# Routed attention and an MLP mixer on one core: attention in units of four heads by half the queries

## The chip, the cores and the metric

The kernel runs on one core of a Trainium2 chip. A core has a matrix engine (TensorE, PE in the profile), a vector engine (VectorE, DVE), a scalar engine (ScalarE, ACT), GpSimd (POOL), and SyncE (SP), which issues most transfers here. Operands lie in an on-chip memory of 128 partitions. Matmuls write to eight banks of a second memory (`ps` in the code), from which DVE and ACT read. The metric is the device time of one execution in microseconds (us). The kernel before takes 802.99 us, the median of three runs from 802.93 to 803.22.

## The reference

There are two blocks, one behind the other. The first is attention with routing: B = 4 batches, H = 8 heads, S = 768 positions, head dimension 64, 16 centroids for each head. Each query and key is assigned to its best centroid, and a query sees only the keys of its own cluster:

```python
q_assign = np.argmax(np.einsum('bhsd,hcd->bhsc', q_n, c_n), axis=-1)
k_assign = np.argmax(np.einsum('bhsd,hcd->bhsc', k_n, c_n), axis=-1)
mask = q_assign[:, :, :, None] == k_assign[:, :, None, :]
scores = scale * np.matmul(q, k.transpose(0, 1, 3, 2))
scores = np.where(mask, scores, -1000000000.0)
scores = scores - np.max(scores, axis=-1, keepdims=True)
attn = np.exp(scores)
attn = attn / (np.sum(attn, axis=-1, keepdims=True) + 1e-09)
return np.matmul(attn, v).astype(np.float32)
```

The heads are put side by side to x, 768 positions by 512 channels for each batch. The second block is an MLP mixer: `h = relu(x^T w_tok1) w_tok2` over positions, `u = x + h^T`, then `u + relu(u w_ch1) w_ch2` over channels. The weights come in 64-bit floats; the kernel gets them as pairs of 32-bit words and rounds them itself.

## The kernel before, in words

**Work and its order.** Everything is one straight program, and all tiles are stretches of one large buffer, `arena`. The program is first recorded as operations (class `Program`, lines 72 to 226), each with its cost, with what it reads and writes, and with the engines that may do it. Then `plan` lays out an order for every engine: PE keeps the order in which its operations were recorded; every other engine takes the operation that is ready and has the earliest due time, by the costs in the code. SP's transfers are ordered in the same way. On the chip each engine then goes through its own list strictly in order, and waits for semaphores where an operation needs another engine's result. So a planner's cost that differs from the chip's time changes no order, only who waits.

**Attention** goes in 16 units (`pair(m)`, line 1282), one for two heads. Both heads of a pair lie beside each other: 64 partitions each.

- *Load.* `load_qkr` fetches queries and keys, `part_qk` (ACT, line 870 through `halves`) splits them into high and low halfwords, SP transposes these by DMA (line 905), and `join_qk` (ACT) puts them together into `Ts`: head dimension on partitions. The first three pairs are transposed on PE instead (`turn_qk`).
- *Route* (line 1068): PE multiplies by the centroids (four column groups of 32), DVE takes the largest of each 16 (lines 1085 to 1090), ACT makes of it rows of 0 and 1 and rows of 0 and minus a large number, and counts hits (line 1094). Through a small DRAM tile these rows become the mask operands `Ms`, so that one bf16 matmul adds a large negative number to each score outside the cluster.
- *Scores* (line 1147): 12 chunks, each one key tile of 128 keys by half the queries (384), for both heads. For each head there is one f32 matmul (64 rows by 128 columns of the array, the two heads in two row groups) and one bf16 matmul with the mask; they leave the result in two banks. ACT takes the exponential of both heads at once (line 1190, 768 numbers in each partition) into `exs`. Three pairs of banks take turns. DVE adds the six key tiles up in two sums (`tt`, line 880, 1536 numbers).
- *Values* (line 1218): for each of six key tiles 16 f32 matmuls: two heads, two halves of the head dimension, and four groups of 32 queries, each group in a column group of its own (line 1207). The sums of the exponentials come in the same way (`sums`).
- *Finish* (line 1246): DVE turns sums and values back (lines 1249 and 1263), takes the reciprocal and multiplies.

The operations of PE in a pair follow each other as scores, four key tiles of values, the route of the pair after the next, two more key tiles with the sums.

**The mixer** follows: token products by a Strassen-like scheme (seven products in place of eight), then channel products by two levels of it. Their weights are rounded in 31 pieces (`weight_round`, line 1306: DVE lines 1326 to 1336, and `tt`), which may begin at START + STEP x n us, lie beside the attention, and go to DRAM. A check of ranges at the end reads the weights once more (`weights_in_range`, ACT line 1863) and counts (`check`). A second, general path is taken only if the check fails.

The code as it stands, with its line numbers:

Of the kernel before, what the change touches and what calls it, by code (L numbers as in the profile page):

```python
# [9 lines left out]
F32 = mybir.dt.float32  # L10
# [9 lines left out]
C = 16  # L20
# [40 lines left out]
HOLD = {"DVE": 0.15}  # L61
# [5 lines left out]
START, STEP = 14, 13  # L67


class Op:  # L70
    __slots__ = ("opts", "fn", "preds", "succs", "left", "ready", "end", "due", "seq", "eng", "lat", "bytes", "after", "port", "first_lat", "mode")


class Program:
# [10 lines left out]
    def add(self, opts, fn, rd=(), wr=(), size=None, after=0.0, mode=None):  # L85
# [3 lines left out]
        o.lat, o.mode = 0.0, mode  # L89
# [27 lines left out]
    def run(self):  # L117
# [602 lines left out]
def kernel(  # L720
# [38 lines left out]
    wdm = [dram.tile([P, HS], BF16, name=f"wdm{i}") for i in range(2)]  # L759
# [19 lines left out]
    araw = buf(75, [768, 2], U32)  # L779
# [4 lines left out]
    vs = [buf(15 + 3 * i, [2, NJ, D]) for i in range(3)]  # L784
    Ts = [buf(24 + 6 * i, [NQK, P]) for i in range(3)]
    Ms = [buf(42 + 3 * i, [2, S], BF16) for i in range(2)]
    M0 = buf(102, [2, S], BF16)
    heads = Buf(arena, 330, [2])
    msc0 = Buf(arena, 332, [2, 2])
    exs = [buf(48 + 6 * i, [2, S]) for i in range(6)] + [buf(96, [2, S])]  # L790
    es = [buf(84 + 6 * i, [2, S]) for i in range(2)]
    denT = buf(105, [HS])
    rt = [buf(106.5 + 1.5 * i, [HS]) for i in range(3)]

    qkr = buf(9, [2, 2, NJ, D])
    qka = [buf(3 + 3 * i, [2, NJ, 2, D], U16) for i in range(2)]
    qkt = [buf(111 + 3 * i, [NQK, P], U16) for i in range(2)]
    rb = buf(117, [HS], BF16)
    nsq = buf(118, [P])
    mxs = buf(118.5, [32])  # L800
    hits = Buf(arena, 672, [32])

    O = buf(119, [8, 2, 2, W])
    Os = buf(127, [4, 7, W])
    raws = [buf(134 + 4 * i, [WMAX, 2], U32) for i in range(3)]
    tmps = [[buf(146 + 6 * i + 2 * n, [WMAX], U32) for n in range(3)] for i in range(2)]
# [86 lines left out]
    def vec(fn, c, rd, wr):  # L893
        return g.add({"DVE": c - 0.08}, lambda e: fn(), rd, wr)
# [8 lines left out]
    def transpose(dst, src, rd, wr, kb):  # L903
        return g.add(
            {"SP": ISSUE}, lambda e: nc.sync.dma_start(dst, src, transpose=True), rd, wr,
            (1.3 * kb * 1024, 512),
        )


# [12 lines left out]
    def load_qkr(m, after=0.0):  # L922
# [1082 lines left out]
```

## Time and profile before

| | |
|---|---|
| median of three runs | 802.99 us |
| the profiled execution | 803.35 us |
| its span | 801.3 us |
| granted clock of PE, mean | 0.998 |
| PE busy | 785.5 us, 98% |
| DVE busy | 663.9 us, 83% |
| ACT busy | 468.0 us, 58% |
| POOL busy | 189.6 us, 24% |
| transfers | 143.70 MB, 70.0% of 16 DMA engines on the main queue |

A line of groups reads: code line, engine, operation, what is written and read, partitions by numbers of the form, count; then busy time and the mean of one in nanoseconds, then idle time before it with what ended it. PE's matmuls overlap, so the mean of one is longer than its share of the time. An f32 matmul of the code leaves two records (two passes), each with a weight load (PEld), a bf16 matmul one. The chain that ended last is given as start, length, and what was done.

### The profile page before, as it was taken

The page shows a single profiled execution, that of the slowest core. Times are in us where ns is not written, and L with a number is a line of the kernel's source. Part 1 is how long each engine was busy: PE and PEld are TensorE (multiplying, and loading weights), DVE is VectorE, ACT ScalarE, POOL GpSimd, SP SyncE. Part 2 cuts the span into 40 slices and gives each one's busy share as a digit, 9 for nine tenths or more (in the row PEclk, how much of TensorE's full clock was granted, in tenths as well). Part 3 has the DMA queues.
Part 4 walks back from the last instruction along what each step waited for, and adds up shares of the span by engine and source line. Part 5 has one row for each costly group of instructions (what it writes and reads, how often), then busy time and mean ns, then how long its engine had stood idle before and what let it go on. Part 6 is the DMA issues. An engine that isn't in the chain of part 4 may idle for free.

```text
span 801.3 us, 15484 instructions
## 1 busy us (share of the span) xinstructions
PE 785.5 (98%) x6063; PEld 467.3 (58%) x6063; DVE 663.9 (83%) x863; ACT 468.0 (58%) x615; POOL 189.6 (24%) x185
## 2 busy tenths in 40 slices
PE   8999999999999999999999999999999999999995
PEld 5566666666666666544555555555555555555553
DVE  6888788999999999999998767899852677799962
ACT  5588888888888875699623235434537605401332
POOL 0000000000000000001255599700285289810000
PEclk9999999999999999999999999999999999999999
DMA  8466666998999875689967855557987943333765
GB/s 186 159 170 152 146 159 170 219 211 186 227 234 202 188 217 129 146 159 203 196 182 209 246 182 177 185 179 199 253 246 199 262 120 101 103 103 98 178 155 136
DMA packets 264883, 143.70 MB, mean 179 GB/s; under 512 B 184160, under 2 KB 260704, under 8 KB 264800
## 3 DMA queue, kind: packets, MB, share of 16 engines
q1 hardware_dynamic: 262432, 141.83, 70.0%
q8 instruction: 50, 0.82, 0.4%
q10 hardware_dynamic: 2368, 0.79, 0.4%
q14 instruction: 33, 0.27, 0.1%
HBM read 91.95 MB, written 28.61 MB: 150 GB/s over the span
## 4 chain that ended last, share of the span: by engine, by line
PE 83%; DVE 10%; ACT 4%; issue 2%; POOL 0%; DVEq 0%; POOLq 0%; ACTq 0%
PE ps L841 68%; PE ps L1207 15%; DVE arena L880 7%; ACT arena L870 2%; ACT arena L1190 1%; DVE arena L1330 1%; DVE arena L1333 0%; DVE arena L1263 0%; DVE arena L1336 0%; ACT arena L860 0%; ACT arena L887 0%; DVE arena L1326 0%; DVE arena L1249 0%; DVE arena L862 0%; DVE arena L1085 0%
## 5 line engine op out<-in xcount | busy, mean ns | idle before, releaser
L841 PE MATMUL ps<-arena 128*128 128x384 f32 (+5 forms) x2735 | 641.3, 462 | 7.9 <-DVE arena L862 2.1
L841 PEld LDWEIGHTS ps<-arena 128*128 128x128 f32 (+1 forms) x2351 | 341.5, 185 | 252.8 <-issue 58.6
L880 DVE TENSOR_TENSOR arena<-arena 128x256 f32<-128x256 f32 (+6 forms) x340 | 354.1, 1062 | 22.9 <-ACT arena L1190 14.2
L880 POOL TENSOR_TENSOR arena<-arena 128x384 f32<-128x384 f32 x179 | 188.9, 1085 | 514.8 <-DVE arena L880 390.9
L880 DVE TENSOR_TENSOR arena<-ps,arena 128x384 f32<-128x384 f32 (+3 forms) x227 | 189.1, 843 | 88.7 <-PE ps L841 85.2
L870 ACT COPY arena<-arena 128x768 uint16<-128x768 uint16 x223 | 191.4, 948 | 47.9 <-DMA arena<-arena 22.3
L1190 ACT ACTIVATE arena<-ps 128x768 f32<-128x768 f32 x192 | 153.0, 810 | 32.4 <-PE ps L841 30.7
L1207 PE MATMUL ps<-arena 128*32 128x192 f32 (+1 forms) x3328 | 151.1, 339 | 0.0
L1207 PEld LDWEIGHTS ps<-arena 128*32 128x32 f32 x3328 | 106.5, 110 | 48.0 <-issue 20.3
L860 ACT COPY arena<-ps 128x1152 f32<-128x1152 f32 (+2 forms) x42 | 30.8, 738 | 105.4 <-PE ps L841 105.4
L887 ACT ACTIVATE arena<-arena 128x1152 f32<-128x1152 f32 (+1 forms) x38 | 40.2, 1076 | 55.5 <-DVE arena L880 54.1
L1863 ACT ACTIVATE arena<-arena 128x768 f32<-128x768 f32 x40 | 38.8, 969 | 56.4 <-DMA arena<-in_moe_w_tok_dram 30.7
L841 PEld LDWEIGHTS <-arena 64*128 64x128 bf16 x384 | 19.2, 94 | 25.0 <-DVE arena L1117 0.6
L1094 ACT ACTIVATE arena<-arena 128x384 bf16<-128x384 f32 x16 | 11.3, 708 | 19.7 <-ACT arena L870 9.5
L1336 DVE SCALAR_TENSOR_TENSOR arena<-arena 128x512 f32<-128x512 uint32 (+1 forms) x31 | 21.2, 684 | 0.7
L1330 DVE SCALAR_TENSOR_TENSOR arena<-arena 128x512 uint32<-128x512 uint32 (+1 forms) x31 | 20.7, 669 | 0.8
L1263 DVE STREAM_TRANSPOSE arena<-ps 128x768 f32<-128x768 f32 x16 | 15.6, 975 | 1.1 <-PE ps L1207 1.0
L1333 DVE TENSOR_SCALAR arena<-arena 128x512 uint32<-128x512 uint32 (+1 forms) x31 | 14.2, 457 | 0.5
L1085 DVE STREAM_TRANSPOSE arena<-ps 128x384 f32<-128x384 f32 x16 | 9.3, 580 | 4.7 <-PE ps L841 4.6
L1326 DVE TENSOR_SCALAR arena<-arena 128x512 uint32<-128x512 uint32 (+1 forms) x31 | 12.5, 403 | 0.0
L1249 DVE STREAM_TRANSPOSE arena<-ps 128x384 f32<-128x384 f32 x16 | 9.2, 577 | 3.0 <-PE ps L1207 2.9
L1090 DVE STREAM_TRANSPOSE arena<-arena 128x384 f32<-128x384 f32 x16 | 9.3, 578 | 0.6
(58 smaller groups left out, 49.6 us busy)
## 6 DMA issues: line engine op xcount, KB each, us to landing
arena<-wd SPq DMA_DIRECT2D x196, 192.0 KB, 2.5
wd<-arena SPq DMA_DIRECT2D x84, 224.0 KB, 3.7
arena<-in_moe_w_ch_dram SPq DMA_DIRECT2D x48, 256.0 KB, 4.8
arena<-in_moe_w_ch_dram SPq DMA_DIRECT2D x16, 768.0 KB, 4.4
arena<-in_v_dram SPq DMA_DIRECT2D x16, 384.0 KB, 5.1
out_dram<-arena SPq DMA_DIRECT2D x14, 384.0 KB, 3.8
arena<-in_k_dram SPq DMA_DIRECT2D x13, 384.0 KB, 3.9
arena<-in_q_dram SPq DMA_DIRECT2D x13, 384.0 KB, 4.3
```

The lines of the kernel that those rows point to most:

```text
L841: nc.tensor.matmul(dst, lhsT=lhsT, rhs=rhs, start=start, stop=stop, tile_position=pos, is_transpose=tr, skip_group_check=True,)
L860: nc.scalar.copy(out=dst, in_=src)
L870: nc.scalar.copy(out=dst, in_=src)
L880: (nc.vector if e == "DVE" else nc.gpsimd).tensor_tensor(out=dst, in0=a, in1=b, op=op)
L887: nc.scalar.activation(out=dst, in_=src, func=ACT.Relu)
L1190: lambda e, ex=ex, s=s, u=u: nc.scalar.activation(out=ex.ap[:, :, u * HS : (u + 1) * HS], in_=ps[:, 2 * s : 2 * s + 2, 0:HS], func=ACT.Exp ...
L1207: nc.tensor.matmul(dst, lhsT=lhsT, rhs=rhs, start=start, stop=stop, tile_position=pos, skip_group_check=True,)
L1263: lambda: nc.vector.transpose(out=x.ap[:, :, cols].rearrange("p j (c d) -> p c j d", d=32), in_=ps[:, 6:8, 0:HS],),
L1330: vec(lambda: nc.vector.scalar_tensor_tensor(out=TT, in0=hi, scalar=0xC0000000, in1=hh, op0=ALU.bitwise_and, op1=ALU.bitwise_or), 0.14 + 0 ...
L1333: vec(lambda: nc.vector.tensor_scalar(out=hh, in0=TT, scalar1=0xFF800000, scalar2=None, op0=ALU.bitwise_and), f, T.k(), h.k())
L1336: vec(lambda: nc.vector.scalar_tensor_tensor(out=ll, in0=lo, scalar=float(2.0**-52), in1=hh.bitcast(F32), op0=ALU.mult, op1=ALU.mult,), 0. ...
L1863: lambda e, i=i, func=func, bias=bias, n=n, hi=hi: nc.scalar.activation(out=hi, in_=hi, func=func, bias=bias, accum_out=wsum.ap[:, i, n : ...
```

## The change

It changes the units of attention from the third on. Pairs 0 and 1 stay as they are. Units 2 to 15 (`quad(t)`) each hold four heads of a batch and half of the queries; two units (w = 0 and 1) share the four heads n = t // 2.

- Queries and keys come as pieces (`load_piece`): half the positions of four heads, in rows of 768 bytes in place of 1536. `part_piece` also sorts them into blocks: 32 partitions for each head, the two halves of the head dimension (z) behind each other. Pieces 2 and 3 are sorted by copies and turned on PE (`turn_piece`, 12 transposes each), where before pair 2 alone was. Four tiles `Ts` in place of three.
- Scores (`scores_quad`): for a key tile, four row groups of 32, one head in each: two f32 matmuls (z = 0 and 1) and one bf16 mask matmul for each head, 384 queries, in four banks. Two exponentials follow, for two heads each, of the same size as before. Two sets of four banks take turns.
- Route (`route_quad`): once for four heads and all positions, in tiles of 64 rows by 32 columns, 16 matmuls, at the fifth key tile of even units. DVE's steps are done once on 768 numbers in place of twice on 384; the rows of the mask are now made by DVE, and ACT only counts. One transfer out and four in make a mask for four heads.
- Values (`values_quad`): for a key tile 32 matmuls of 96 columns in place of 16 of 192; they fill two banks of the half that the unit does not use for its last scores; sums go to a third bank there. `finish_quad` turns these out in two transposes.
- The planner's model: transfers cost by their packets, ACT may hold back 0.2 us for a more urgent operation, an operation can be given an earlier due time. Weight pieces may start every 9 us in place of 13; from the nineteenth piece on two load buffers in place of three, and one set of temporaries.
- The last range check has two load buffers in place of one, and `check` stands before the second group's first channel product.

```diff
-HOLD = {"DVE": 0.15}
+HOLD = {"DVE": 0.15, "ACT": 0.2}
...
-START, STEP = 14, 13
+START, STEP = 14, 9
...
-            o.bytes = size[0] * (1.2 if size[1] < 512 else 1.0)
+            o.bytes = BUS * size[0] / size[1] * (11 + 0.037 * size[1]) / 16e3
...
-                    o.due = min([s.due - 0.15 - lat for s in o.succs], default=total) - c
+                    o.due = min([s.due - 0.15 - lat for s in o.succs], default=total) - c - o.early
...
+    vq = [buf(15 + 6 * i, [4, NJ, D]) for i in range(2)]
+    Ts = [buf(at, [NQK, P]) for at in (39, 45, 27, 33)]
+    Ms = [buf(51 + 3 * i, [2, S], BF16) for i in range(2)]
+    exs = [buf(at, [2, S]) for at in (81, 87, 69, 75, 93, 57, 63)]
+    es = [buf(99 + 6 * i, [2, S]) for i in range(2)]
+    rt = [buf(112.5 + 3 * i, [2, HS]) for i in range(2)]
...
+    def load_piece(e, t, after=0.0):
+        n, w = divmod(e, 2)
+        b, hq = divmod(n, 2)
         for i, a in ((0, k), (1, q)):
             dma(
+                t.ap[:, 4 * i : 4 * i + 4].rearrange("p h j d -> p h (j d)"),
+                a[b, 4 * hq : 4 * hq + 4].rearrange("h (p j) d -> p h (j d)", p=P)[
+                    :, :, HJ * D * w : HJ * D * (w + 1)
+                ],
...
+    def turn_piece(e, banks):
+        t, R, T = rawq[e % 2], blk, Ts[e % 4]
+        src = t.ap.rearrange("p a j (z d) -> p z j a d", z=2)
+        for z in range(2):
...
+                    h.ap[:, z], src[:, z, n], S, qkr.k() + [("exps", e - 4)], h.rows(z, z + 1),
...
+    def join_piece(e):
...
+                    qkt[n].k() + [("exps", e - 3)], T.rows(r, r + NJ),
...
+    def assign(m, banks):
+        n = len(banks)
+        a, o, r = (Buf(arena, z.off, [n * HS], d) for z, d in zip((*rt, rb), (F32, F32, BF16)))
+        ak = a.k() + mxs.k()
+        src = ps[:, banks[0] : banks[-1] + 1 : max(1, banks[-1] - banks[0]), 0:HS]
...
+    def route_quad(n, banks):
+        hq = n % 2
+        parts = []
+        for z in range(2):
+            for p2 in range(2):
+                rows = slice(64 * p2, 64 * p2 + 64)
+                for gr in range(4):
+                    T = Ts[(2 * n + gr % 2) % 4]
+                    parts.append((
+                        ps[32 * gr : 32 * gr + 32, banks[p2], 0:HS], cbq.ap[rows, z, hq],
+                        blocks_of(T)[rows, z, :, 1 - gr // 2], z == 0, z == 1, (64 * p2, 32 * gr),
+                    ))
+        Tk = Ts[2 * n % 4].k() + Ts[(2 * n + 1) % 4].k()
+        mms(parts, 1.29, Tk + cbq.k(), bank(*banks), (64, 32))
+        assign(n + 1, banks)
+        dma(wdm, rb.ap, rb.k(), [("wdm",)], 192, 1536)
+        M = Ms[n % 2]
+        for h in range(4):
+            dma(
+                M.ap[32 * h : 32 * h + C].rearrange("c i (u n) -> c (i u) n", u=2),
+                wdm.rearrange("(g r) a n -> r g a n", g=4)[
+                    C * (h % 2) : C * (h % 2) + C, :, h // 2
+                ],
+                [("wdm",)] + M.k(), [("mq", n % 2, h // 2, h % 2)], 48, 768,
+            )
...
+    def scores_quad(t):
+        nonlocal nex
+        n, w = divmod(t, 2)
+        M, Tq = Ms[n % 2], Ts[t % 4]
+        st = unit[t] = [Buf(arena, exs[(nex + i) % len(exs)].off, [4, HS]) for i in range(NJ)]
+        nex += NJ
+        for i in range(NJ):
+            kw, kj = divmod(i, HJ)
+            Tk = Ts[(2 * n + kw) % 4]
+            s0 = 4 * ((i + t) % 2)
+            def rows(h):
+                return slice(32 * h, 32 * h + 32)
+            for z in range(2):
+                for p2 in range(2):
+                    mms(
+                        [
+                            (
+                                ps[:, s0 + h, 0:HS], blocks_of(Tk)[rows(h), z, kj, 0],
+                                blocks_of(Tq)[rows(h), z, :, 1], z == 0, False, (32 * h, 0),
+                            )
+                            for h in (2 * p2, 2 * p2 + 1)
+                        ],
+                        0.3225, Tk.k() + Tq.k(), bank(s0 + 2 * p2, s0 + 2 * p2 + 1), (32, P),
+                    )
+            for p2 in range(2):
+                mms(
+                    [
+                        (
+                            ps[:, s0 + h, 0:HS], M.ap[rows(h), 1, i * P : (i + 1) * P],
+                            M.ap[rows(h), 0, w * HS : (w + 1) * HS], False, True, (32 * h, 0),
+                        )
+                        for h in (2 * p2, 2 * p2 + 1)
+                    ],
+                    0.081, [("mq", n % 2, p2, h) for h in range(2)] + M.k(),
+                    bank(s0 + 2 * p2, s0 + 2 * p2 + 1), (32, P),
                 )
+            ex = st[i]
+            for p2 in range(2):
+                b0 = s0 + 2 * p2
+                g.add(
+                    {"ACT": 0.70},
+                    lambda e, ex=ex, b0=b0, p2=p2: nc.scalar.activation(
+                        out=ex.ap[:, 2 * p2 : 2 * p2 + 2], in_=ps[:, b0 : b0 + 2, 0:HS],
+                        func=ACT.Exp, scale=SM_SCALE,
+                    ),
+                    bank(b0, b0 + 1),
+                    ex.rows(2 * p2, 2 * p2 + 2)
+                    + ([("exps", t)] if i == NJ - 1 and p2 else []),
+                )
+        add_up(st)
...
+    def values_quad(t, i):
+        V, ex = vq[t // 2 % 2], unit[t][i]
+        b0 = 4 * (t % 2)
+        for p2 in range(2):
+            mms(
+                [
+                    (
+                        ps[32 * gr : 32 * gr + 32, b0 + p2, (2 * h + c) * 96 : (2 * h + c + 1) * 96],
+                        V.ap[:, 2 * p2 + h, i, 32 * c : 32 * c + 32],
+                        tokens(ex.ap[:, 2 * p2 + h], gr),
+                        i == 0 and h == 0 and c == 0, i == NJ - 1, (0, 32 * gr),
+                    )
+                    for h in range(2) for c in range(2) for gr in range(4)
+                ],
+                0.645, V.rows(2 * p2, 2 * p2 + 2) + ex.rows(2 * p2, 2 * p2 + 2), bank(b0 + p2),
+                (P, 32),
+            )
...
+    def finish_quad(t, bk):
+        n, w = divmod(t, 2)
+        b, hq = divmod(n, 2)
+        x, rcp = xs[b], rcps[t % 2]
+        vec(lambda: nc.vector.transpose(out=denT.ap, in_=ps[:, bk, 0:HS]), 0.57, bank(bk), denT.k())
...
+        js = slice(HJ * w, HJ * w + HJ)
+        b0 = 4 * w
+        for p2 in range(2):
+            cols = slice((2 * hq + p2) * P, (2 * hq + p2 + 1) * P)
+            vec(
+                lambda p2=p2, cols=cols: nc.vector.transpose(
+                    out=x.ap[:, js, cols].rearrange("p j (c d) -> p c j d", d=32),
+                    in_=ps[:, b0 + p2, 0:HS],
+                ),
+                0.57, bank(b0 + p2), x.rows(HJ * w, HJ * w + HJ, cols.start, cols.stop),
+            )
...
+    def ahead(t):
+        if t >= 1 and t + 3 < NP:
+            join_piece(t + 3)
+        if t + 4 < NP:
+            part_piece(t + 4)
+            if t + 5 < NP:
+                load_piece(t + 5, qkr)
     def pair(m):
         scores(m)
+        ahead(m)
         for i in range(NJ):
             if i == NJ - 1:
                 sums(m, 5)
             values(m, i)
+            if m == 0 and i == 3:
+                turn_piece(2, (0, 1, 2))
+        if m == 0:
+            turn_piece(3, (3, 4, 0))
         finish_x(m, 5)
         if m == 0:
+            route_quad(1, (1, 2))
+        else:
+            load_vq(2)
+    def quad(t):
+        scores_quad(t)
+        ahead(t)
+        for i in range(NJ):
+            if i == 4 and t % 2 == 0 and t + 2 < NP:
+                route_quad(t // 2 + 1, (3, 7))
+            if i == NJ - 1:
+                sums(t, 4 * (t % 2) + 2)
+            values_quad(t, i)
+        finish_quad(t, 4 * (t % 2) + 2)
+        if t % 2 and t + 3 < NP:
+            load_vq((t + 3) // 2)
...
-        raw, (h, T, low) = raws[npiece % 3], tmps[npiece % 2 if npiece < 22 else 0]
+        raw, (h, T, low) = raws[npiece % (3 if npiece < 18 else 2)], tmps[npiece % 2 if npiece < 18 else 0]
...
+                araw = araws[n % 2]
...
     for m in range(NP):
-        pair(m)
+        if m < 2:
+            pair(m)
+        else:
+            quad(m)
...
     channel1(0)
     channel2(0)
+    check()
     channel1(1)
-    check()
     channel2(1)
```

More of the change, by code (lines that the diff above doesn't have):

```diff
@@ L66 @@
 SELF = 0.13
-START, STEP = 14, 13
+START, STEP = 14, 9
 class Op:
-    __slots__ = ("opts", "fn", "preds", "succs", "left", "ready", "end", "due", "seq", "eng", "lat", "bytes", "after", "port", "first_lat", "mode")
+    __slots__ = ("opts", "fn", "preds", "succs", "left", "ready", "end", "due", "seq", "eng", "lat", "bytes", "after", "port", "first_lat", "mode", "early")
 class Program:
@@ L758 @@
     wd2 = dram.tile([7, 7, P, 3, P], F32, name="wd2")
-    wdm = [dram.tile([P, HS], BF16, name=f"wdm{i}") for i in range(2)]
+    wdm = dram.tile([P, 2, HS], BF16, name="wdm")
     wdt1 = dram.tile([P, NJ * DTOK], F32, name="wdt1")
```

278 lines of the change are left out of this document (171 added, 107 removed).

## The prediction

> **What bounds the kernel now.** I read the page first (busy times, then the chain that ended last), then the chain in one pair of heads, then the timelines of TensorE (PE), ScalarE (ACT) and VectorE (DVE) beside it, and last the places where PE is not the bound.
>
> ```profile
> span 801.3 us, 15484 instructions
> ...
> PE 785.5 (98%) x6063; PEld 467.3 (58%) x6063; DVE 663.9 (83%) x863; ACT 468.0 (58%) x615; POOL 189.6 (24%) x185
> ...
> PE 83%; DVE 10%; ACT 4%; issue 2%; POOL 0%; DVEq 0%; POOLq 0%; ACTq 0%
> ```
>
> The profiled run took 803.35 us: this span and 2.05 us around it. It lies 0.36 us above the median of 802.99. The chain is PE for 83%, so PE's own work per pair is what counts. One pair of heads in the chain (start, us, what):
>
> ```profile
> 216.46 9.89 PE ps L841 x72
> 226.35 5.34 PE ps L1207 x128
> 231.69 0.65 PE ps L841 x8
> 232.34 3.89 PE ps L1207 x80
> 236.23 0.84 PE ps L841 x3
> ```
>
> From score to score a pair takes 236.23 - 216.46 = 19.77 us: scores 9.89, four key tiles of values 5.34, the route of a later pair 0.65, two key tiles of values and the sums 3.89. PE never pauses in it. The same line's matmuls, counted in a window inside the values (us, PE busy and count, PEld busy and count):
>
> ```profile
> 206.60:211.80 5.20, 5.20 (x128) 3.98 (x128) 1.00 0.75 170
> ```
>
> 128 records in 5.20 us are 40.6 ns each (an f32 matmul leaves two records). Four column groups run side by side, so a 192-column record lasts 4 x 40.6 = 162 ns. The sums are 3.89 - 64 x 0.0406 = 1.29 us for 16 records of 384 columns, 81 ns each, so one lasts 323 ns: time goes with columns. A chunk of scores (two heads, 384 queries, one key tile) is (9.89 - 0.2)/12 = 0.807 us: two f32 records of 0.323 in each of two row groups, and 0.162 left for the mask matmul (bf16). The 0.2 is entry and change of tile shape; the seam into the values is 5.34 - 5.20 = 0.14.
>
> **The change, part by part.**
>
> *Scores.* Four row groups of 32 rows: a key tile takes, for four heads, two halves of the head dimension x two f32 records x 0.323 = 1.29, and one mask pass 0.162: 1.452 us. Before, the same heads and queries took two chunks, 1.614. Per unit of six key tiles this is 8.71 instead of 9.69; 14 of 16 units are of the new kind. This assumes that four row groups run side by side as fully as two do (0.807 shows that) and as four column groups do (40.6 x 4). A page of the Trainium skill speaks against it: "TensorE: Matmul & The Clock Gate", "Measured speedup vs the span model", gives 3.07 times for four row tiles. By that figure, as an estimate, a key tile would take 1.452 x 4 / 3.07 = 1.89 us and the run about 37 us more. The window above has four column groups at full rate, so I do not take it.
>
> Can ACT follow? It has to give 12 exponentials per unit as before.
>
> ```profile
> 20.93 2.89 ACT L1190 ACTIVATE arena<-ps 128x768 f32<-128x768 f32 x4
> ...
> 217.51 9.75 ACT L1190 ACTIVATE arena<-ps 128x768 f32<-128x768 f32 x12 [1.61 <-PE ps L841]
> 227.16 6.75 ACT L870 COPY arena<-arena 128x768 uint16<-128x768 uint16 x8
> ```
>
> In the first pair, with work waiting, four take 2.89, so one follows another in (2.89 - 0.81)/3 = 0.69 us, 0.81 being the length of one. In the steady pair they come at (9.75 - 0.81)/11 = 0.81, which is PE's pace. So ACT needs 12 x 0.69 = 8.3 us, less than 8.71, and with eight copies (6.75) and one accumulation of 1 us 16 of a unit's 19. PE stays the bound, but the banks are tighter: all eight hold two key tiles. The first exponential starts 217.51 - 216.39 = 1.12 after the scores (216.39 by PE's timeline), about 0.37 after the mask starts. The second of a tile is 0.69 later and lasts 0.81: it frees its banks 1.87 after the mask, while row groups 2 and 3 want them 0.162 + 1.452 = 1.61 after it. These two groups trail by 0.26, paid once per unit, since the groups keep their own pace. Scores: 8.71 + 0.2 + 0.26 = 9.2 instead of 9.89, -0.7 x 14 = -9.7 us. Between four copies and the last exponential that the new ACT order puts behind them, the sums still have about 1 us to spare.
>
> *Values.* 16 records of 192 columns per head pair and key tile become 32 of 96 for four heads and half the queries: 384 records a unit instead of 192, at half the columns. Twice 162.4 is 2 more than 323, so a record has some 2 ns that do not go with columns: one of 96 would last (162.4 + 2) / 2 = 82 ns, a quarter of it 20.6, and the unit 7.91 us instead of 7.80: +0.11 x 14 = +1.5. Nothing in the trace goes so fast. Nearest is the start of the values:
>
> ```profile
> 206.52 0.48 PEld L1207 LDWEIGHTS ps<-arena 128*32 128x32 f32 x16 [0.48 <-issue]
> ```
>
> Sixteen weight loads within 0.48, the last lasting 0.11: 24.7 ns apart, held back there by the streams, not by issue. Bounds: 20.3 (no fixed part), and 40.6 (as now, whatever the columns). I take 20.6, because 384 and 192 columns already scale exactly. Instructions are fetched by DMA in packets of 0.82 MB / 50 = 16 KB; 1.09 MB for 15,484 instructions is 70 bytes each, so some 240 in a packet:
>
> ```profile
> q8 instruction: 50, 0.82, 0.4%
> ...
> q14 instruction: 33, 0.27, 0.1%
> ```
>
> At 20.6 ns for a load and a matmul, a packet lasts 2.5 us in the values; 10 us of scores refill the buffer, so I put no wait there.
>
> *Route.* Before: 13 pairs have 0.65 inside the values. Now six units have 32 records of 384 columns over eight tiles of 64 x 32: 32 x 0.323 / 8 = 1.29, and two seams of 0.14, since this shape differs from the values': 6 x 1.57 - 13 x 0.65 = +1.0.
>
> *Start.* Pieces 2 and 3 are turned on PE, where one pair was before.
>
> ```profile
> 25.21 9.30 PE L1207 MATMUL ps<-arena 128*32 128x192 f32 x208
> 34.44 1.53 PE L841 MATMUL ps<-arena 128*128 128x128 f32 x12
> 36.84 0.85 PE L841 MATMUL ps<-arena 128*32 128x384 f32 x8 [0.87 <-DVE arena L862]
> 38.38 0.92 PE L841 MATMUL ps<-arena 64*128 64x384 f32 x4 [0.69 <-DVE arena L1085]
> ```
>
> Another 12 turns 1.53, two seams 0.28, a doubled route +0.65, and DVE's turn of two banks instead of one in the wait at 38.38 (0.98 against 0.58 us for such a transpose): +0.4. ACT places the first mask behind the accumulation now: +0.4. Sum +3.2. The added copies into blocks and the centroids' four lie beside PE's turns, which wait for the loads.
>
> *Finish.* The banks of a unit's values are now wanted by the next unit's second key tile. DVE turns them out in two transposes.
>
> ```profile
> 215.97 0.49 PE L1207 MATMUL ps<-arena 128*32 128x192 f32 x5
> ...
> 216.53 0.98 DVE L1263 STREAM_TRANSPOSE arena<-ps 128x768 f32<-128x768 f32 x1 [0.24 <-PE ps L1207]
> ...
> 324.80 8.95 PE L1207 MATMUL ps<-arena 128*32 128x192 f32 x200
> ...
> 337.32 0.94 DVE L1263 STREAM_TRANSPOSE arena<-ps 128x768 f32<-128x768 f32 x1
> ```
>
> In the steady pair DVE comes 0.07 after PE ends (216.46); two transposes of 0.57 end 1.2 later, and the second key tile starts 1.58 after the scores begin: 0.3 to spare. At the end of attention DVE is 337.32 - 333.75 = 3.6 late, and nothing waits for it there before; now the next unit would. DVE's load per unit is as before, near the limit:
>
> ```profile
> 256.00:275.70 19.70, 19.70 (x290) 12.29 (x290) 18.79 (x28) 17.15 (x22) 0.00 (x0) 1.00 0.91 178
> ...
> 390.00:420.00 30.00, 28.71 (x86) 15.62 (x84) 29.82 (x56) 9.09 (x9) 12.67 (x12) 1.00 0.76 181
> ```
>
> (Third and fifth fields: PE's busy time and, two on, DVE's 18.79 of 19.70.) I put 2.0 us for such waits, bounds 0 and 14 x 1.
>
> *Transfers.* SP issues as many loads, in rows of 768 bytes; masks go out in one and in by four per two units. Cover: the route is two units ahead of its scores, some 20 us. If it goes, PE waits for a mask about 5 us once per four heads. I cost them at nothing. The weight pieces may start every 9 us instead of 13; in the DVE order 25 pieces stand before attention's end, 24 before.
>
> *After attention.* The second row of the last fence shows DVE full at 29.82 of 30 while PE loses 1.3; between 390 and 420 us the chain runs through DVE. The new order has one add of 1,536, one of 512 and two of 384 columns less there, some 3.4 us of DVE's time; I take half, -1.5 (bounds 0 and -4). The earlier check and the second buffer for the range check lie beside PE's channel work: nothing.
>
> Sum: -9.7 + 1.5 + 1.0 + 3.2 + 2.0 - 1.5 = -3.5, and pair 1's route already counted. 803.35 - 3.5 is 799.9; on the median's footing 799.5. I say 800.0.
>
> **Rivals.**
> 1. *The values are bound by records, not columns* (slower). Place: the 384 records a unit. Price: each ns above 20.6 is 384 x 14 = 5.4 us. At the 24.7 of the weight loads +22, 822 us; at 40.6 it would be 907. It decides from 21.2 ns on, where the gain is gone. For it: no row is faster. Against it: exact scaling so far. The same page of the Trainium skill ("Wait - 56ns, not 53.3ns?") has a floor of about 25 ns from start to start of matmuls; by that figure, as an estimate, 824 us. No run here shows it.
> 2. *ACT or DVE becomes the bound at the banks* (slower). If exponentials keep 0.81, scores take 1.12 + 8 x 0.81 + 1.45 + 0.2 = 9.3 to 9.8, and DVE late by 0.6 per unit costs 8: 808 to 815 us. For it: two tiles of banks, the late transposes. Against: 0.69, and 0.07 in the steady pair.
> 3. *Four row groups do not overlap more than two* for the masks: the mask costs 0.32 per key tile, the 13.6 us of it stay, and 800 becomes 813. The change would not do what it says.
> 4. *More gain*: no waits at the banks and after attention: 800 - 2 - 3 = 795, with a cheaper start 792.
>
> **How the numbers follow.** A measurement can tell 0.2% (1.6 us) from no change. Forecast 0.55 (own range 795 to 806: faster 0.40, same 0.10, slower 0.05); rival 1 0.18; rival 2 0.13; rival 3 0.07; rival 4 0.07. Faster 0.47, same 0.10, slower 0.43. The range 794 to 836 leaves out rival 1 beyond 27 ns (0.08), and the low end of rival 4 (0.05).
>
> **What would show it.** The chain in a unit: scores 9.2 us; 384 value records in 7.9; period 18.6 without a route and 20.1 with one. Exponentials 0.69 to 0.73 apart. The first scores of pair 1 at about 41.6 us, attention's end about 331 to 332. Rival 1: value records over 21 ns. Rival 2: PE's idle time before scores released by ACT or by DVE's transposes. Rival 3: key tiles of 1.6 us with ACT idle. Wrong altogether: instruction fetches stalling PE, or DVE falling behind over several units.

## The result, and the profile after

The changed kernel takes 831.37 us (median, 829.15 to 833.43), the kernel before beside it 802.96 us. The ratio is 1.0355, 95% interval 1.0319 to 1.039: slower, where the prediction said 800.0 us. The profiled execution took 829.52 us, its span is 827.7 us.

Four lines of the page of the changed kernel answer to those of the kernel before: its head, PE's busy time, the queue of instructions, and the chain that ended last.

```profile
span 827.7 us, 22392 instructions
...
PE 797.5 (96%) x9547; PEld 516.7 (62%) x9547; DVE 665.1 (80%) x862; ACT 452.7 (55%) x602; POOL 189.1 (23%) x185
...
q8 instruction: 77, 1.26, 0.6%
...
PE 83%; DVE 9%; issue 4%; ACT 3%; DMA 1%; POOL 0%; SPq 0%; DVEq 0%; POOLq 0%
```

The line of the queue gives packets, MB and the share of 16 DMA engines. There are 6,908 more instructions than before (22,392 - 15,484), and this queue moves 0.44 MB more (1.26 - 0.82): 64 bytes each, so a packet of 16 KB holds 256. In the chain, "issue" has gone from 2% to 4%. Issue is time in which an engine waits for nothing that the profile shows. PE's waits, by what ended them (us in total, times, longest):

```profile
PE ps L920 <- issue: 17.4, 21, 2.2
PE ps L847 <- DVE arena L886: 1.9, 4, 0.8
```

No other engine keeps PE waiting for long; the first line has no counterpart before (0.3 us in one place). Where it lies is seen in the table of stretches, here the fourteen units from the third on (from their first score to the first turn behind attention), first in the kernel before and then in the changed one. The columns are start:end, length, then busy time and count of PE, PEld, DVE, ACT and POOL, PE's clock, DMA share and GB/s.

```profile
58.29:333.68 275.39, 275.39 (x4020) 172.29 (x4016) 250.46 (x341) 224.61 (x288) 0.00 (x0) 1.00 0.78 186
```

```profile
60.28:363.89 303.61, 285.97 (x7477) 217.04 (x7473) 256.22 (x343) 206.42 (x271) 0.00 (x0) 1.00 0.74 167
```

| stage | before | after | difference | forecast |
|---|---|---|---|---|
| to the first score of unit 2 | 58.29 | 60.28 | +2.0 | +2.6 |
| the fourteen units | 275.39 | 303.61 | +28.2 | -4.6 |
| behind attention (span less 333.68 and 363.89) | 467.6 | 463.8 | -3.8 | -1.5 |

(The forecast has the route of pair 1, -0.65, in the first line.) The whole loss is in the fourteen units. The chain inside the values of two of them, with start, length and what was done:

```profile
181.55 0.78 issue
182.33 2.85 PE ps L920 x128
185.18 1.16 issue
186.34 3.82 PE ps L920 x99
```

```profile
188.99 13.91 PE ps L920 x304
202.90 0.43 issue
203.33 3.92 PE ps L920 x128
207.24 1.46 issue
208.70 3.81 PE ps L920 x124
212.51 1.57 issue
214.08 1.05 PE ps L920 x15
```

The gaps come 128 records apart (the chain leaves some records out; PE's timeline counts 128 from 208.70 too): 128 matmuls and their 128 weight loads are 256 instructions, one packet. The 21 gaps of the list of waits, and two more of 0.1 us, lie multiples of 128 records apart (one record is missing from the trace), and where the count falls into scores or into the route, the gap is there:

```profile
82.44 15.65 PE L920 MATMUL ps<-arena 32*128 32x384 f32 x384 [0.19 <-issue]
98.97 3.81 PE L920 MATMUL ps<-arena 128*32 128x96 f32 x128 [0.88 <-issue]
103.80 16.22 PE L920 MATMUL ps<-arena 128*32 128x96 f32 x384 [1.02 <-issue]
120.57 20.06 PE L920 MATMUL ps<-arena 64*32 64x384 f32 x512 [0.55 <-issue]
```

The packets of the instruction queue stand in the trace too. In these 23 gaps the packet ahead of PE's next record begins 0.6 to 3.1 us after the 256 instructions before it have begun, takes 0.9 to 1.3 us, and PE goes on 1.3 to 1.7 us after its end (at 186.34: packet from 184.03 to 184.99). So these are waits for instructions.

From start to start of the stretches in the two chains it is 186.34 - 182.33 = 4.01, 5.37 and 5.38 us; this is called a round below. The stretches of 3.92 and 3.81 us hold records of the route or of the sums, which are longer. The one of 2.85 us holds values alone, of which 0.25 is the last one's own length: (2.85 - 0.25)/127 = 20.5 ns from one to the next. So the array takes narrow records as fast as was forecast, and then has no instruction to go on with. The same instructions grouped by form, over the fourteen units:

```profile
L920 PE MATMUL ps<-arena 32*128 32x384 f32 x1344 | 136.1, 494 | 0.7 <-issue 0.7
L920 PE MATMUL ps<-arena 128*32 128x96 f32 x5376 | 126.3, 247 | 16.4 <-issue 16.1
```

Taken from start to start, the 5,376 value records last 138.2 us; by their columns, at 0.323 us for 384 in one of four groups, they should last 108.5. That is 29.7 us lost; the kernel before loses 2.6 by the same reckoning. (The list of waits has less, because PE counts as busy until the last record before a gap has ended.)

The scores are the second loss. ACT's timeline shows one unit, its eleven exponentials ahead of a copy:

```profile
147.95 2.97 ACT L1377 ACTIVATE arena<-ps 128x768 f32<-128x768 f32 x4 [3.03 <-PE ps L920]
151.20 2.92 ACT L1377 ACTIVATE arena<-ps 128x768 f32<-128x768 f32 x4 [0.28 <-PE ps L920]
154.38 2.47 ACT L1377 ACTIVATE arena<-ps 128x768 f32<-128x768 f32 x3 [0.27 <-PE ps L920]
```

After each fourth one, so once for each turn of the two sets of banks, ACT waits 0.28 us for PE. PE needs 9.68 us from a unit's first score to its first value, not 9.2:

```profile
189.57:199.25 9.68, 9.68 (x124) 6.28 (x121) 9.46 (x15) 7.37 (x10) 0.00 (x0) 1.00 1.06 255
```

### The profile page after: what moved, and what is told of

The parts are those of the page before. It is cut to its first block, busy times and chain, and to the rows that moved or that the text cites. A ratio compares the mean times of both kernels' runs of the same rounds, so it can differ in the third digit from the quotient of the medians.

```text
span 827.7 us, 22392 instructions
## 1 busy us (share of the span) xinstructions
PE 797.5 (96%) x9547; PEld 516.7 (62%) x9547; DVE 665.1 (80%) x862; ACT 452.7 (55%) x602; POOL 189.1 (23%) x185
## 3 DMA queue, kind: packets, MB, share of 16 engines
q8 instruction: 77, 1.26, 0.6%
## 4 chain that ended last, share of the span: by engine, by line
PE 83%; DVE 9%; issue 4%; ACT 3%; DMA 1%; POOL 0%; SPq 0%; DVEq 0%; POOLq 0%
PE ps L847 47%; PE ps L920 36%; DVE arena L886 7%; ACT arena L876 2%; DMA arena<-in_moe_w_ch_dram 1%; DVE arena L868 1%; ACT arena L866 0%; DVE arena L1569 0%; DVE arena L1575 0%; ACT arena L2103 0%; ACT arena L893 0%; DVE arena L1154 0%; DVE arena L1572 0%; DVE arena L1257 0%; DVE arena L1565 0%
## 5 line engine op out<-in xcount | busy, mean ns | idle before, releaser
L847 PE MATMUL ps<-arena 128*128 128x384 f32 (+5 forms) x1627 | 491.4, 478 | 7.1 <-DVE arena L886 1.9
L847 PEld LDWEIGHTS ps<-arena 128*128 128x128 f32 (+2 forms) x1579 | 284.2, 189 | 210.1 <-issue 26.4
L886 DVE TENSOR_TENSOR arena<-arena 128x1536 f32<-128x1536 f32 (+6 forms) x333 | 351.3, 1078 | 27.9 <-ACT arena L1377 16.2
L920 PE MATMUL ps<-arena 128*32 128x96 f32 (+5 forms) x7920 | 306.6, 310 | 17.6 <-issue 17.4
L920 PEld LDWEIGHTS ps<-arena 128*32 128x32 f32 (+2 forms) x7584 | 223.0, 123 | 86.1 <-issue 42.3
L1377 ACT ACTIVATE arena<-ps 128x768 f32<-128x768 f32 x168 | 126.2, 810 | 93.5 <-PE ps L920 92.7
L866 ACT COPY arena<-ps 128x1152 f32<-128x1152 f32 (+3 forms) x50 | 34.1, 693 | 121.8 <-PE ps L847 121.7
L1488 DVE STREAM_TRANSPOSE arena<-ps 128x384 f32<-128x384 f32 x28 | 16.1, 577 | 9.2 <-PE ps L920 8.3
L1317 ACT ACTIVATE arena<-ps 128x768 f32<-128x768 f32 x24 | 18.5, 811 | 5.0 <-PE ps L847 4.7
L920 PEld LDWEIGHTS <-arena 32*128 32x128 bf16 x336 | 15.0, 93 | 6.9
L1154 DVE STREAM_TRANSPOSE arena<-ps 128x768 f32<-128x768 f32 (+1 forms) x9 | 8.0, 884 | 5.8 <-PE ps L920 4.7
L1157 DVE TENSOR_REDUCE arena<-arena 128x48 f32<-128x768 f32 (+1 forms) x9 | 7.8, 864 | 0.3
```

Source lines behind the costliest of these rows:

```text
L847: nc.tensor.matmul(dst, lhsT=lhsT, rhs=rhs, start=start, stop=stop, tile_position=pos, is_transpose=tr, skip_group_check=True,)
L866: nc.scalar.copy(out=dst, in_=src)
L886: (nc.vector if e == "DVE" else nc.gpsimd).tensor_tensor(out=dst, in0=a, in1=b, op=op)
L920: nc.tensor.matmul(dst, lhsT=lhsT, rhs=rhs, start=start, stop=stop, tile_position=pos, skip_group_check=True,)
L1317: lambda e, ex=ex, s=s, u=u: nc.scalar.activation(out=ex.ap[:, :, u * HS : (u + 1) * HS], in_=ps[:, 2 * s : 2 * s + 2, 0:HS], func=ACT.Exp ...
L1377: lambda e, ex=ex, b0=b0, p2=p2: nc.scalar.activation(out=ex.ap[:, 2 * p2 : 2 * p2 + 2], in_=ps[:, b0 : b0 + 2, 0:HS], func=ACT.Exp, scale ...
```

## The experiments

Two theories. F: PE gets its instructions in packets of 256, the next one not earlier than about 4 us after it has begun the last, and the values use one in some 2.6. S: the scores are held up because heads 0 and 1's exponential is released late. Their rivals: what was lost went with columns, banks, loads or the planner's settings, or with each record, or the round of a bank is simply as long as it is.

### Half the instructions, the same columns

```diff
+            both = ex.ap[:, 2 * p2 : 2 * p2 + 2].rearrange("p h n -> p (h n)")
...
-                        ps[32 * gr : 32 * gr + 32, b0 + p2, (2 * h + c) * 96 : (2 * h + c + 1) * 96],
-                        V.ap[:, 2 * p2 + h, i, 32 * c : 32 * c + 32],
-                        tokens(ex.ap[:, 2 * p2 + h], gr),
-                        i == 0 and h == 0 and c == 0, i == NJ - 1, (0, 32 * gr),
+                        ps[32 * gr : 32 * gr + 32, b0 + p2, c * 192 : (c + 1) * 192],
+                        V.ap[:, 2 * p2, i, 32 * c : 32 * c + 32], tokens(both, gr),
+                        i == 0 and c == 0, i == NJ - 1, (0, 32 * gr),
                     )
-                    for h in range(2) for c in range(2) for gr in range(4)
+                    for c in range(2) for gr in range(4)
```

> The changed kernel with the values of four heads in records of 192 columns instead of 96: half the instructions, the same columns, the same banks and order. Leaves out: the second and fourth head's own V (both heads of a pair are multiplied by the first one's V), so its output is not the reference's. Theory F (instruction fetch: PE gets a packet of 256 instructions, 128 f32 records, no oftener than about every 4.0 us, where the values use one in 2.8): the waits of PE for its own instructions (17.4 us in the changed kernel) go to under 1, the values' excess over their columns (29.7 us by its trace) falls to 2 or less, total 831.4 - 28 = 803 (800 to 806). Rival C (the time of the values was lost to something that goes with columns, banks or transfers: DVE's transposes, the new order of loads, the weights' 9 us): total unchanged, 828 to 834.

Measured: 800.07 us, 31.3 less than the changed kernel; ratio to the kernel before 0.9966 (0.9954 to 0.9979). In its fourteen units PE is never idle:

```profile
60.23:334.85 274.62, 274.62 (x4789) 183.22 (x4785) 254.27 (x343) 205.50 (x270) 0.00 (x0) 1.00 0.80 183
```

Waits for instructions are gone from PE's list, and the values' excess is 3.4 us. Rival C falls: columns, banks, transfers, the planner's settings and DVE's work are the same here. But a loss for each record would give the same, so the next run asks for the form of the curve.

### The same in every second key tile

```diff
                     for c in range(2) for gr in range(4)
-                ],
+                ] if i % 2 else [
...
+                    for h in range(2) for c in range(2) for gr in range(4)
+                ],
```

(Against the run before it: the even key tiles have the changed kernel's records of 96 columns again.)

> The changed kernel with records of 192 columns in every second key tile only (1, 3 and 5), so a quarter of the values' instructions goes; leaves out what the run before it leaves out, in these tiles. Theory F is not linear: what counts is whether 256 instructions in a row last 4.0 us, and alternating tiles make them last 3.5. With a model that charges max(0, 4.0 - duration) for each 256 instructions of a unit, the stalls fall from 31.0 to 6.5 us: total 831.4 - 24.5 = 807 (804 to 812). Rival R (each record of 96 columns costs some ns too many, whatever its neighbours are): linear, half of what the first run gains, some 817.

Measured: 805.62 us (ratio 1.0034, 1.002 to 1.0049), 25.8 less than the changed kernel. Half the edit gives 82% of the gain. F's model had 24.5; a loss for each record had half. PE's waits in this run:

```profile
PE ps L920 <- issue: 2.9, 3, 1.5
```

### The values of the kernel before in records of 96 columns

```diff
-                    ps[32 * gr : 32 * gr + 32, 6 + h, c * HS // 2 : (c + 1) * HS // 2],
-                    V.ap[:, h, i, 32 * c : 32 * c + 32], tokens(ex.ap[:, h], gr),
+                    ps[32 * gr : 32 * gr + 32, 6 + h, (2 * c + u) * 96 : (2 * c + u + 1) * 96],
+                    V.ap[:, h, i, 32 * c : 32 * c + 32],
+                    tokens(ex.ap[:, h], gr)[:, 3 * u : 3 * u + 3],
...
+                for h in range(2) for c in range(2) for u in range(2) for gr in range(4)
```

> One part alone in the kernel before: its values in records of 96 columns instead of 192 (twice the instructions, the same columns and the same result), nothing else changed. Theory F: 16 pairs, the same model gives 33 us of stalls at 4.0 us per packet, and 16 x 0.11 for the fixed part of a record: 803 + 35 = 838 (830 to 846), with waits of PE for its own instructions after every 128 records of the values. Rival C (the loss comes with the units of four heads, their banks, masks or loads): 803 to 806.

Measured: 833.09 us, ratio 1.0381 (1.0363 to 1.0398). The kernel before, with nothing but more instructions for the same columns, is as slow as the changed one, and has the same wait:

```profile
PE ps L1207 <- issue: 14.8, 18, 2.4
PE ps L841 <- DVE arena L862: 2.1, 3, 0.9
```

With these three runs and the packets of the trace F is shown: what counts is how many instructions come in a row, not the units of four heads.

### The masks of heads 0 and 1 earlier in PE's order

```diff
             part(0, 0)
             part(0, 1)
             part(1, 0)
-            part(1, 1)
             mask(0)
+            part(1, 1)
             mask(1)
```

(`part(z, p2)` are the f32 matmuls of one half of the head dimension for heads 2 x p2 and 2 x p2 + 1, `mask(p2)` their masks.)

> The changed kernel with one step of PE's order moved in each key tile of scores: the masks of heads 0 and 1 ahead of the second half of heads 2 and 3, not behind it. Nothing is left out. Theory S (scores take 9.67 us a unit and not 9.2, because heads 0 and 1's exponential is released only when the matmul ahead of their mask in PE's order, that of heads 2 and 3, has ended, so that the lag of heads 2 and 3 adds to the round of a bank): scores 9.2 to 9.3 us, 14 x 0.4 = 5.6 less: 825.8 (824 to 828). Rival (the round of a bank is bound by the two exponentials themselves, or PE cannot pass the waiting row groups): scores stay at 9.67, total 829 to 833.

Measured: 831.79 us, no change in the total. But the step did what S says. The same unit on ACT, and a unit's scores on PE:

```profile
147.03 8.84 ACT L1384 ACTIVATE arena<-ps 128x768 f32<-128x768 f32 x12 [3.83 <-PE ps L920]
```

```profile
188.22:197.62 9.40, 9.40 (x124) 6.79 (x121) 8.77 (x15) 7.64 (x11) 0.00 (x0) 1.00 1.08 238
```

Twelve exponentials without a wait, in the time of eleven, and a unit's scores take 9.40 us instead of 9.68. From start to start, the scores of the fourteen units last 134.4 us instead of 138.1, but values, routes and sums 2.5 us more, and PE's waits for instructions are 18.5 us instead of 17.4: two thirds of the gain were handed on to the packets. The units are 1.2 us shorter (302.44 us against 303.61), and behind attention 1.4 us are given back (465.2 against 463.8). The expected time missed because F was left out of it, so the two edits were run together.

### Both edits

The diff is the first and the fourth together.

> Both edits together: values in records of 192 columns (leaving out the second and fourth head's own V, as above) and the masks of heads 0 and 1 moved ahead. The step of the masks alone shortened a unit's scores from 9.67 to 9.39 us in its trace and the total not at all. If that gain was handed to the stalls for instructions (each packet takes its round, however short the work is), it shows here, where there are no stalls: 800.1 - 14 x 0.28 = 796.2 (795.5 to 797.5). Rival (the scores' time isn't on the path that ends the unit: ACT or DVE sets the period): 799.5 to 800.8.

Measured: 797.29 us, ratio 0.9932 (0.9915 to 0.9948), 2.8 less than with the wide records alone. Scores and values of two units in the table of stretches:

```profile
197.13:206.52 9.39, 9.39 (x124) 6.72 (x120) 8.94 (x13) 7.63 (x11) 0.00 (x0) 1.00 1.12 176
206.52:215.75 9.23, 9.23 (x210) 6.66 (x209) 9.06 (x14) 8.79 (x12) 0.00 (x0) 1.00 0.70 121
215.75:225.14 9.39, 9.39 (x124) 6.79 (x120) 8.53 (x14) 7.63 (x11) 0.00 (x0) 1.00 1.08 255
225.14:235.96 10.82, 10.82 (x242) 7.04 (x241) 10.40 (x13) 7.85 (x10) 0.00 (x0) 1.00 0.74 175
```

The periods are 18.62 us without a route and 20.21 with one. The fourteen units:

```profile
60.41:330.69 270.28, 270.28 (x4788) 190.70 (x4784) 254.77 (x342) 203.80 (x270) 0.00 (x0) 1.00 0.80 186
```

They take 4.3 us less than with wide records alone; behind attention some 2.5 of it are given back (465.9 us to the end of the span, against 463.4) in the two profiled executions, which are 1.6 us apart where the medians are 2.8.

### Fewer transfers beside it

```diff
-            dma(part(raw.ap), src, [], raw.k((2 * c, 2 * (c + w))), w, 512, after)
+            dma(part(raw.ap)[0:8], src[0:8], [], raw.k((2 * c, 2 * (c + w))), w, 512, after)
```

> The changed kernel with the loads of the mixer's weights cut to 8 of 128 partitions (the rest of the buffers is zeroed once), all instructions kept. Leaves out: 15/16 of these weights, so the mixer's output is not the reference's. Question: why a packet of instructions takes 4.0 to 5.4 us from the start of the one before it, where its own transfer takes 0.9 to 1.3. Theory Q (the packet waits behind other transfers: in the one stall that a trace shows with idle DMA engines, the round was 3.45 us): with a third of the traffic in attention gone the round falls to 3.5 to 4.0 and the stalls from 30 to 12 to 22 us: total 813 to 823. Rival (the round is a fixed time): stalls stay at 27 to 31, total 828 to 833.

Measured: 830.0 us, ratio 1.0329 (1.0307 to 1.0351). The DMA share over the fourteen units is 0.60 (0.74 in the changed kernel) and the rate 134 GB/s (167), so a fifth of the traffic went and not a third. The stalls hardly move; the values lose 27.8 us over their columns instead of 29.7:

```profile
63.79:365.16 301.37, 285.33 (x7476) 217.40 (x7472) 256.33 (x343) 206.20 (x271) 0.00 (x0) 1.00 0.60 134
```

```profile
PE ps L920 <- issue: 14.8, 23, 1.3
```

So theory Q missed. It rested on one stall of the run with the masks moved; PE's timeline and the stretch between the two starts are

```profile
245.27 2.84 PE L920 MATMUL ps<-arena 128*32 128x96 f32 x128 [0.83 <-issue]
248.72 3.77 PE L920 MATMUL ps<-arena 128*32 128x96 f32 x115 [0.61 <-issue]
```

```profile
245.27:248.72 3.45, 2.84 (x128) 2.62 (x129) 3.28 (x7) 3.45 (x5) 0.00 (x0) 1.00 0.05 14
```

With the DMA engines idle (0.05) the round was 3.45 us, the shortest that these traces show between two such gaps; beside transfers it is mostly 4.0 to 5.4. It is not the only one: the kernel before with narrow records has three rounds of 3.45 or 3.46 us, at shares of 0.15, 0.02 and 0.04. But in the run with fewer transfers one took 4.00 at 0.05 (from 250.09) and one 3.73 at 0.02 (from 315.97), so idle DMA engines do not make the round short by themselves. A fixed round is refuted as well: all 43 rounds between two such gaps, in five runs, lie within 0.04 us of 3.45 + n x 0.274 us, with n from 0 to 8. Even 3.45 is longer than 128 narrow records. What sets the steps, and what part other transfers have in them, stays open.

### The product the other way round

The exponentials are the weights and V moves, so that 288 instructions do what 768 do. Only the core of the edit is shown; V's buffers get a column of ones, and its loads and the finish change with it.

```diff
-                        V.ap[:, 2 * p2 + h, i, 32 * c : 32 * c + 32],
-                        tokens(ex.ap[:, 2 * p2 + h], gr),
+                        ps[:, b0 + p2, (HJ * h + j) * (D + 1) : (HJ * h + j + 1) * (D + 1)],
+                        ex.ap[:, 2 * p2 + h, j * P : (j + 1) * P], V.ap[:, 2 * p2 + h, i],
```

> The changed kernel with the masks moved ahead and the values' product the other way round: the exponentials (128 keys by 128 queries) are the weights and V with a column of ones (65 columns) moves, so a unit has 144 records in place of 384, the row sums come with them (DVE's adds of exponentials, the matmuls of the sums and the transposes out of PSUM go), and the result is token-major. The same result is computed. 288 instructions a unit cannot starve PE. If a record goes by its columns (65 x 0.84 = 55 ns): values 7.9 us and no sums (1.3 and a seam less): 796 - 14 x 1.3 = 778, less a few us after attention where DVE is full (770 to 785). If the load of 128 x 128 weights sets the pace, nearest the transposes' 109 ns: values 15.7 us, 796 + 14 x 6.4 = 886.

Measured: 905.17 us, ratio 1.1271 (1.1251 to 1.1291). The values of one unit, grouped by form:

```profile
L920 PE MATMUL ps<-arena 128*128 128x65 f32 x142 | 16.1, 275 | 0.0
```

(16.1 - 0.275)/141 = 112 ns a record, close to the transposes' 109 and twice what 65 columns need. The weight loads run without a break beside them, 80 in 9.0 us:

```profile
L920 PEld LDWEIGHTS ps<-arena 128*128 128x128 f32 x80 | 9.0, 192 | 0.5 <-ACT arena L1389 0.5
```

So f32 weights of 128 columns set the pace, the second of the two expected cases. Its time, 886 us, was 19 too low: the fourteen units last 375.36 us, 105.1 more than with both edits, so 7.5 a unit and not 6.4 (from start to start, values 16.3 us and scores 9.9). A cure for the instructions is not free.

### The rest of the change, in the kernel before

First only the edits behind attention (two buffers for the range check, its loads at 418, `check` ahead of the second group's first channel product, `early` 20); then the planner's settings with them (the costs of the transposes by DMA follow the third line too):

```diff
-HOLD = {"DVE": 0.15}
+HOLD = {"DVE": 0.15, "ACT": 0.2}
...
-START, STEP = 14, 13
+START, STEP = 14, 9
...
-            o.bytes = size[0] * (1.2 if size[1] < 512 else 1.0)
+            o.bytes = BUS * size[0] / size[1] * (11 + 0.037 * size[1]) / 16e3
```

> The kernel before with only those edits of the change that lie after attention: two buffers for the range check of the weights in place of one, its loads from 418 us of the plan, the check of the sums ahead of the second half's first channel product with its own buffer, its last sum 20 us earlier. Nothing left out. From attention's end to the end of the span the kernel before takes 801.3 - 333.7 = 467.6 us, the changed one 827.7 - 363.9 = 463.8. If these edits give that: 802.7 - 3.8 = 799 (798 to 800.5). Rival (they lie beside PE's work; the 3.8 come from another order of DVE's work, left by the planner's settings and the longer attention): 802 to 803.3.

> The run before it and the planner's settings of the change too: weight pieces every 9 us in place of 13, ACT's hold of 0.2, transfers costed by packets. Nothing left out; attention keeps its pairs of heads, 192 columns and two row groups. If the settings move DVE's work into attention and so free it behind: 798 to 800 even where the run before stays at 802.7. If they fill DVE within attention (18.79 of 19.70 us busy before) PE waits there: 804 to 812.

Measured: 801.98 us for the first (ratio 0.9983, 0.9974 to 0.9993), 1.3 us under the kernel before beside it and not 3.8, and 799.46 us for the second (0.9953, 0.9939 to 0.9967). The fourteen units of the second:

```profile
58.73:334.12 275.39, 275.39 (x4020) 172.31 (x4016) 260.99 (x370) 224.67 (x288) 0.00 (x0) 1.00 0.86 204
```

They last as long as before to the hundredth, with 260.99 us of DVE's work in place of 250.46, and behind attention 463.5 us are left of the span of 797.6, in place of 467.6. DVE had room in attention, and work done there is missing where DVE sets the end. Which of the three settings does it was not tried one by one. This kernel leaves nothing out and takes 0.5% less than the kernel before (interval 0.3% to 0.6%).

## Why the prediction was wrong

**Instructions: the step that failed.** "A packet lasts 2.5 us in the values; 10 us of scores refill the buffer, so I put no wait there." The first half was right (2.6 us for 128 records at 20.5 ns); the second took the buffer for larger than it is. In the changed kernel's fourteen units no packet begins more than 0.6 us before the 256 instructions ahead of it do: only the next 256 are fetched ahead, however long the scores last. A unit's values are 768 instructions, three packets, and each may begin only one round after the last. They lose 29.7 us over their columns where the kernel before loses 2.6: 27.1 more, and 1.5 was forecast. The trace before could not show it, since there a packet lasts 5.2 us in the values and no gap ever opens. But then the cost was unknown and needed an upper bound. The prediction named such stalls only under "wrong altogether", with no price and no chance. The Trainium skill, "Runtime: NRT & Kernel Launch", "Instruction fetch mechanics", has blocks of 256 instructions, the next one fetched while the last is executed, and calls the cost of crossing one mostly hidden. The size agrees with the gaps 128 records apart; hidden it is not here, with 17.4 us of waits in PE's list.

**Scores: the mechanism was half right.** Four row groups do run fully side by side: in the changed kernel a unit's first two key tiles follow each other by 1.45 us (their second passes start at 60.71 and 62.16 in the first unit), as forecast (1.452). With both edits a unit's scores take 9.39 us where 9.2 was forecast, and the periods are 18.62 and 20.21 where 18.6 and 20.1 were. In the kernel as changed it is 9.68, a gain of 0.2 for each unit and not 0.7. The step that failed is "paid once per unit, since the groups keep their own pace". They share one order: heads 0 and 1's exponential comes only when the matmul ahead of their mask in that order, of the trailing heads 2 and 3, is through, so the lag returns in each turn of the banks. The run with the masks moved shows that the order of these two steps makes the difference; that it is the end of that matmul which counts is read from the times, not tried by itself.

**Values' rate, route, start: right.** 20.5 ns a record (forecast 20.6). The page of the Trainium skill cited in the prediction, "TensorE: Matmul & The Clock Gate", has in "Wait - 56ns, not 53.3ns?" a floor of about 25 ns from start to start; the 128 records in 2.85 us, in four column groups, are under it. The route adds 20.21 - 18.62 = 1.59 us (1.57). Pair 1's scores behind DVE's turn start at 41.17 (41.6):

```profile
41.17 9.95 PE L847 MATMUL ps<-arena 64*128 64x384 f32 x70 [0.83 <-DVE arena L1154]
```

**Finish, transfers, after attention.** The 2.0 us for DVE's late transposes did not come: with both edits PE is busy without a break through fourteen units. Behind attention it was -3.8 instead of -1.5, inside its bound of -4; in the kernel before, the planner's settings make most of such a gain (466.7 us behind attention with the late edits alone, 463.5 with the settings), without fewer columns.

**The rivals.** Rival 1 gave a time near the measured one (822 us at 24.7 ns) for a wrong reason, so by luck: the mean from start to start is indeed 25.7 ns (138.2 us for 5,376), but it is 20.5 ns with long gaps between; records are not slow, they are missing. Rival 2 was right in its place, the banks, and in the scores (9.68 us, within its 9.3 to 9.8); the 8 us for a late DVE did not come, so its price was too high. Rival 3 is refuted: 9.39 us leaves no room for a mask of 0.32 in each key tile. Without the two failed steps the sum holds: 797.29 us were measured with both undone, against 799.5. That run leaves out half of the V, so it shows that the other terms were right and is no kernel to use; no run here has the units of four heads in wide records with the right result.

## What to carry to other kernels

Count instructions as a resource of their own: on PE here 256 of them, 128 f32 records with their weight loads, must last about 4 us (the rounds here are 3.45 to 5.65), or PE starves however fast the array is. Splitting a matmul into narrower ones with the same columns is free only while that holds, and a gain elsewhere on PE is handed in good part to the same wait. Where a resource has never been short in the trace at hand, its cost is unknown, not zero.

## What was not expected of the hardware

- Where PE starves, it gets its next 256 instructions 3.45 to 5.65 us after it has begun the last 256, in steps of 0.274 us, though such a packet's own transfer takes about 1 us (0.6% of 16 engines' 827.7 us, over 77 packets). The same columns in 192-wide records run without a wait.
- f32 records of 96 columns in four column groups follow each other in 20.5 ns, where 20.2 go with their columns (0.323 us for 384, in four groups).
- f32 weights of 128 columns take 112 ns a load where the moving side has 65 columns; the loads of 32 columns keep up with 20.5 ns in four groups.
